# The passage between two mixtures of experts: code order, a split moved to VectorE, and drains of GpSimd

## The chip, the cores and the metric

The program runs on one core of one Trainium2 chip. The metric is the device time of one execution in microseconds (us). The kernel before took 1118.88 us in the median of three runs (1117.98 to 1119.69).

TensorE (PE in the profile, PEld for its weight loads), VectorE (DVE), ScalarE (ACT) and GpSimd (POOL) compute; SyncE (SP) issues the plain loads and stores; GpSimd issues the indirect ones, which take each row's address from a table on chip.

## The reference

Three layers follow one another. An attention with pooled keys and values makes 4608 tokens of 512 numbers. A first mixture of 8 experts sends each token to one expert by the largest of 8 logits. A second mixture does the same with its own weights and a bias per modality. An expert is two matrix products with a ReLU between them.

```python
e_idx = np.argmax(logits, axis=1)
...
for e in range(E):
    mask = e_idx == e
    h = np.maximum(x[mask] @ w1[e], 0.0)
    ye = h @ w2[e]
    out[mask] = gate_w[mask, None] * eom[mask, e, None] * ye
```

## The kernel before, in words

**Tokens and blocks.** Attention writes each token as a row into `xs1`, in the region of its expert. The first mixture (`mixture(1, ...)`) then works on blocks of 256 rows of one expert. How many blocks there are depends on the data: at least SMIN = 18, at most SMAX = 25. It scatters its results into `xs2` by the second mixture's expert, and the second mixture (`mixture(2, ...)`) works on blocks of `xs2` and scatters rows into `out`. In the profiled execution mixture 1 has 22 blocks (0 to 21) and mixture 2 has 19.

**A block** is `one(s)`. All products are made of three: weights and activations are each split into a high part (W1H, W2H, xH, HH) and a rest (W1L, W2L, xL, HL). `first_layer` makes eight groups of twelve matmuls, one per 128 columns of the hidden layer; after each two groups ScalarE writes HH[kk] (L772) and VectorE writes HL[kk] (L773). `second_layer` then runs 24 matmuls for each half of 128 tokens (L825). With its last argument true (`apart`) it runs all HH x W2H first, then HH x W2L for the first half of the hidden layer, then HL x W2H, then the rest of HH x W2L; without it, the three products of one group follow one another. A block with at most 128 tokens takes `first_layer_half` instead. ScalarE weighs the result (`weigh`, L828).

**The end of a token in mixture 1.** VectorE takes dot products with the second gate (`dots`, L853) and chooses the expert (`choose`, L868 to L881, which ends with the one-hot `oh`). `place` counts ranks with three small matmuls (L886 to L888) and works out the row (L895 to L902). `scatter` sends the rows with GpSimd's indirect DMA (L907). These steps run one block behind.

**Weights.** When the expert changes, SyncE loads raw weights into R1 and R2 ahead of time. `split1` makes W1H and W1L (ScalarE, VectorE, L192 and L193); W2H is made by ScalarE (L1062) and W2L by GpSimd (`low2`, L839, four pieces of 256 columns per tile).

**Blocks that may come.** From block 18 on, each block stands inside an `If` on a flag read from the tables, nested in the block before it (`rest`, L1092 to L1103). Its `Else` is `end(s - 1)`. So the code of all possible blocks comes first, and the eight copies of `end` stand behind them. Where both branches of an `If` advance semaphores by different amounts, the shorter one makes up for it; on GpSimd this is INC_SWDGE_SEM for indirect DMAs that were not issued.

**The passage** is `end(s)` (L1082). It splits W2 for mixture 2's first block, three tiles with ScalarE and GpSimd (`split2`, L841) and the last one in `rest` of `begin` (L974 to L976) with ScalarE and VectorE. It chooses and places the last block's tokens and runs the first layer of mixture 2's first block. `first_layer` takes a tuple `between` for this: `here` is called after group number `after` (7 of 0 to 7 in the passage), ahead of that pair's results, and `then` after the results of pair `after // 2`. `here` places and scatters the last tokens and makes counts (L222 to L228); `then` makes the block table (L160 to L189) and issues the load of block 1. The rest of block 0 of mixture 2, from its second layer on, stands in `go_on2`, behind all the copies of `end`.

The order of instructions on each engine is the order in which the program writes them. The program schedules by hand and adds semaphores where data is shared.

Of the kernel before, what the change touches and what calls it, by code (L numbers as in the profile page):

```python
# [47 lines left out]
def kernel(ctx, tc, q, k, v, wg, wo, w1, w2, mod, wg2, bias2, v1, v2, out):  # L48
# [717 lines left out]
    def first_layer(xh, xl, between=None):  # L766


        kept = []

        def results(kk, p):
            ACT.activation(HH[kk], p, AF.Relu)  # L772
            DVE.scalar_tensor_tensor(HL[kk], in0=p, scalar=0.0, in1=HH[kk].bitcast(F32), op0=ALU.max, op1=ALU.subtract)  # L773

        after, early, here, then = between or (NF, None, None, None)
        trio = [(W1H, d, xh) for d in range(ND)] + [(W1L, d, xh) for d in (0, 2, 3)] + [(W1H, d, xl) for d in range(ND)] + [(W1L, 1, xh)]
        for kk in range(NF // 2):
            p = pm.tile([P, 2 * BLK], F32, name=f"h{kk}").rearrange("p (c s) -> p c s", c=2)
            for c2 in range(2):
                f = 2 * kk + c2  # L780
                c = f * P
                for n, (W, d, x) in enumerate(trio):
                    PE.matmul(p[:, c2, :], lhsT=W[d][:, c:c + P], rhs=x[:, d, :], start=n == 0, stop=n == 3 * ND - 1)  # L783
                if f == 0 and early:
                    early()
                if f == after:
                    here()
                    for k2, p2 in kept:
                        results(k2, p2)
            if early and 2 * kk + 1 < after:  # L790
                kept.append((kk, p))
                continue
            results(kk, p)
            if kk == after // 2:
                then()

    def first_layer_half(xh, xl):
# [37 lines left out]
    def low2(part):  # L835
        for j in part:
            for c in range(2):
                for w in steps(DM):
                    GP.tensor_tensor(W2L[j][:, c, w], R2[j][:, c, w], W2H[j][:, c, w].bitcast(F32), op=ALU.subtract)  # L839

    def split2(part):  # L841
        for j in part:
            ACT.activation(W2H[j], R2[j], AF.Copy)
            low2((j,))

    bc2 = lambda t: t.unsqueeze(2).to_broadcast([P, 2, E])
    c28 = lambda t: t.unsqueeze(1).to_broadcast([P, 2, E])
# [68 lines left out]
    def mixture(m, rows, a1, a2, base, first, after):  # L916
# [44 lines left out]

            return rest

        def begin(part, early, before, of, x):

            def opening():

                before()
                counts(base, of()["eh"], ni, nf)

            def rest():
                f = of()
                if m == 2:
                    ACT.activation(W2H[3], R2[3], AF.Copy)  # L974
                    for c in range(2):
                        DVE.tensor_tensor(W2L[3][:, c], R2[3][:, c], W2H[3][:, c].bitcast(F32), op=ALU.subtract)  # L976
                else:
                    DVE.memset(xg_of(1)[:, 1, DM + 1:DM + 2], float(N))
                flag = lambda c: tc.If(reg(nf[0:1, c:c + 1], [ET.SP], 1) > 0)
                table(base, f["order"], *tabs, m)  # L980
                before = list(placed[f"xs{m}"])
                with flag(FMORE) as more:
                    apart(f"xs{m}", SP.dma_start(rows[ds(reg(nf[0:1, FEND:FEND + 1], [ET.SP], E * REG - P), P), :], dummy))
                    load_block(1, reg(f["ei"][0:1, 1:2], [ET.SP], (E - 1) * REG) + BLK, flag(FHALF2))
                placed[f"xs{m}"] = before
                with more.Else():
                    pads(rows, ni, m)
                    fetch(1)
                placed[f"xs{m}"] = before

            first_layer(*x, between=(part, early, opening, rest))

        def ahead():
            pads(rows, ni, m)
# [5 lines left out]
        def one(s):  # L1000
# [22 lines left out]
                split1()  # L1023
            if s == 0:
                p = pm.tile([P, DM], F32, name="y", bufs=2)
                second_layer(0, p)
                if m == 1:
                    turn_in(1)()
            if m == 1:
# [4 lines left out]
            if m == 1:  # L1034
# [8 lines left out]
                    DVE.tensor_tensor(w[:, 1:E], w[:, 1:E], w[:, 0:1].to_broadcast([P, E - 1, DM]), op=ALU.subtract)  # L1043
                dots(p, S, 0)
            if m == 2:
                write_out(S, 0)
            p1 = pm.tile([P, DM], F32, name="y", bufs=2)
            with half2(s, [ET.PE, ET.Activation, ET.Pool]) if s > 0 else ExitStack():  # L1048
# [11 lines left out]
            with when(s, SPLIT2, [ET.Activation, ET.Pool]):  # L1060
                for j in range(NF // 2):
                    ACT.activation(W2H[j], R2[j], AF.Copy)  # L1062
                low2(range(NF // 2))
            if m == 1 and s > 0:
                scatter()
            if m == 1 and s == SMIN - 2:
                fav["e"] = reg(fav["ei"][0:1, 0:1], [ET.SP], E - 1)
# [13 lines left out]

        def end(s):  # L1082

            split2(range(3))
            choose(RS[s % 2])

            def before():
                place(RS[s % 2], half2(s, [ET.Pool]), "t0")()

            after(NF - 1, None, before, lambda: fav, x_of(s + 1))  # L1090

        def rest(s):  # L1092
            before = {g: list(names) for g, names in placed.items()}
            with tc.If(goes_on[s] > 0) as there:
                one(s)
                if s + 1 < SMAX:
                    rest(s + 1)
                elif m == 1:
                    end(s)
            if m == 1:  # L1100
                placed.update(before)
                with there.Else():
                    end(s - 1)  # L1103

        def go_on():
            for s in range(SMIN):
# [37 lines left out]

    begin2, go_on2 = mixture(2, xs2, v1, v2, base2, lambda: M["xg20"], None)
    begin1, go_on1 = mixture(1, xs1, w1, w2, base1, lambda: xg0, begin2)
    begin1(2, last_but_one, room, lambda: dict(order=order1, ei=ei1, eh=eh1), (xH, xL))
    go_on1()
    go_on2()

# [50 lines left out]
```

## Time and profile before

| | |
|---|---|
| median of three runs | 1118.88 us |
| profiled execution, its own time | 1117.44 us |
| its span in the trace | 1115.7 us |
| TensorE busy | 1066.5 us (96%) |
| VectorE, ScalarE, GpSimd busy | 594.6, 393.8, 334.7 us |
| mean granted clock of TensorE | 0.991 |

The span runs from the first to the last instruction; the 1.7 us between it and the execution's own time lie around it. Busy time counts work on data alone: branches, register loads, semaphores, DRAIN and INC_SWDGE_SEM belong to an engine's sequencer, whose name has a q in the trace (POOLq, PEldq). The granted clock is a share of full speed. Times of instructions are us from the span's start, durations of one are in ns or us as the columns say.

### The profile page before, as it was taken

The numbers are of one execution on the slowest core, as the hardware profiler recorded it, in microseconds if no ns is written. First come the engines' busy times: TensorE is split into PE (matmuls) and PEld (weight loads), VectorE is DVE, ScalarE is ACT, GpSimd is POOL, SyncE is SP. The second block draws the span as 40 slices with busy tenths as digits, with TensorE's granted clock in tenths as the row PEclk, the third lists the DMA queues.
The fourth block names the chain that finished last, engine by engine and source line by source line (L and its number), as shares of the span: only waits on it lengthen the run. The fifth ranks groups of instructions, "written<-read, shape, count | busy, mean of one in ns | idle before, by whom it ended". The sixth has DMA issues, their size and how long they took to land. (4 is left out here: it accounts for less than half of the span.)

```text
span 1115.7 us, 21941 instructions
## 1 busy us (share of the span) xinstructions
PE 1066.5 (96%) x7058; PEld 961.6 (86%) x7058; DVE 594.6 (53%) x1839; ACT 393.8 (35%) x924; POOL 334.7 (30%) x563
## 2 busy tenths in 40 slices
PE   7998989999999999999999989999999999999993
PEld 6998888998888888888888878889998898889982
DVE  6889777768887667679866673211112222111120
ACT  6887872216354215236221151211212512111120
POOL 7566484113757215108312130011000140101000
PEclk9999999999999999999999989999999999999997
DMA  9877455613746114125511005511011211111000
GB/s 345 276 283 250 174 201 189 218 49 123 258 155 225 58 49 161 64 78 163 185 54 41 21 24 177 205 58 58 31 40 39 60 40 39 43 55 40 21 20 22
DMA packets 52096, 128.17 MB, mean 115 GB/s; under 512 B 6957, under 2 KB 10029, under 8 KB 51760
## 3 DMA queue, kind: packets, MB, share of 16 engines
q1 hardware_dynamic: 42928, 97.28, 26.7%
q0 software_dynamic: 8960, 28.47, 6.5%
q8 instruction: 88, 1.44, 0.5%
q14 instruction: 120, 0.98, 0.3%
HBM read 92.51 MB, written 34.27 MB: 114 GB/s over the span
## 5 line engine op out<-in xcount | busy, mean ns | idle before, releaser
L773 DVE SCALAR_TENSOR_TENSOR hl<-h,hh 128x512 fp32r<-128x512 f32 x140 | 95.3, 690 | 368.4 <-ACT hh L772 365.3
L825 PE MATMUL y<-W2H,hh 128*128 128x512 f32 x608 | 235.3, 398 | 2.8 <-ACT W2H L974 2.5
L825 PE MATMUL y<-W2L,hh 128*128 128x512 f32 x608 | 234.6, 395 | 0.5 <-POOL W2L L839 0.5
L825 PE MATMUL y<-W2H,hl 128*128 128x512 f32 x608 | 233.3, 395 | 0.0
L772 ACT ACTIVATE hh<-h 128x512 fp32r<-128x512 f32 x140 | 83.3, 596 | 312.4 <-PE h L783 309.2
L853 DVE CUSTOM_DVE_ANT_0 junk<-y,wg2b 128x512 f32<-128x512 f32 x273 | 169.5, 685 | 8.3 <-ACTq L1060 5.2
L828 ACT ACTIVATE y<-y,xg 128x512 f32<-128x512 f32 x76 | 52.3, 688 | 300.4 <-PE y L825 236.4
L1080 POOL DMA_INDIRECT out_dram<-y,ti x37 | 36.0, 973 | 380.1 <-ACT y L828 258.9
L825 PEld LDWEIGHTS y<-W2H,hh 128*128 128x128 f32 x608 | 114.0, 188 | 28.5 <-ACT W2H L974 2.5
L825 PEld LDWEIGHTS y<-W2H,hl 128*128 128x128 f32 x608 | 114.4, 188 | 26.8
L825 PEld LDWEIGHTS y<-W2L,hh 128*128 128x128 f32 x608 | 114.6, 188 | 26.0 <-POOL W2L L839 1.3
L839 POOL TENSOR_TENSOR W2L<-R,W2H 128x256 fp32r<-128x256 f32 x140 | 99.5, 747 | 84.5 <-ACT W2H L1062 82.2
L783 PE MATMUL h<-xH,W1L 128*128 128x256 f32 x608 | 123.7, 285 | 0.2 <-DVE W1L L193 0.2
L783 PE MATMUL h<-xH,W1H 128*128 128x256 f32 x608 | 100.4, 288 | 4.6 <-issue 3.8
L783 PE MATMUL h<-x2H,W1L 128*128 128x256 f32 x512 | 103.2, 282 | 0.1
L907 POOL DMA_INDIRECT xs<-y,qdi x39 | 39.8, 1020 | 203.3 <-DVE lg L853 190.0
L783 PE MATMUL h<-xL,W1H 128*128 128x256 f32 x608 | 98.5, 285 | 0.0
L783 PEld LDWEIGHTS h<-xH,W1L 128*128 128x128 f32 x608 | 95.8, 193 | 0.4 <-DVE W1L L193 0.4
L783 PEld LDWEIGHTS h<-xH,W1H 128*128 128x128 f32 x608 | 84.7, 194 | 5.0 <-issue 3.8
L783 PEld LDWEIGHTS h<-xL,W1H 128*128 128x128 f32 x608 | 84.6, 194 | 0.0
L783 PE MATMUL h<-x2H,W1H 128*128 128x256 f32 x512 | 83.8, 285 | 0.4 <-ACT x2H L245 0.4
L783 PE MATMUL h<-x2L,W1H 128*128 128x256 f32 x512 | 82.1, 282 | 0.0
(241 smaller groups left out, 1597.1 us busy)
## 6 DMA issues: line engine op xcount, KB each, us to landing
R<-in_w_dram SPq DMA_DIRECT2D x56, 512.0 KB, 4.7
xg<-xs SPq DMA_DIRECT2D x72, 258.0 KB, 2.7
kv<-in_v_dram SPq DMA_DIRECT2D x16, 576.0 KB, 4.5
R<-in_v_dram SPq DMA_DIRECT2D x16, 512.0 KB, 6.3
kv<-in_k_dram SPq DMA_DIRECT2D x14, 576.0 KB, 8.8
qt<-in_q_dram SPq DMA_DIRECT2D x14, 576.0 KB, 10.1
xs<-dummy SPq DMA_DIRECT2D x18, 258.0 KB, 3.5
wraw<-in_w_dram SPq DMA_DIRECT2D x8, 512.0 KB, 4.3
```

Of the source, the lines that this page charges most:

```text
L772: ACT.activation(HH[kk], p, AF.Relu)
L773: DVE.scalar_tensor_tensor(HL[kk], in0=p, scalar=0.0, in1=HH[kk].bitcast(F32), op0=ALU.max, op1=ALU.subtract)
L783: PE.matmul(p[:, c2, :], lhsT=W[d][:, c:c + P], rhs=x[:, d, :], start=n == 0, stop=n == 3 * ND - 1)
L825: PE.matmul(p, lhsT=X[f // 2][:, f % 2, hf * P:(hf + 1) * P], rhs=W[f // 2][:, f % 2, :], start=i == 0, stop=i == 3 * NF - 1)
L828: ACT.activation(S["y"][:, hf, 0:DM], p, AF.Copy, scale=S["xg"][:, hf, DM:DM + 1])
L839: GP.tensor_tensor(W2L[j][:, c, w], R2[j][:, c, w], W2H[j][:, c, w].bitcast(F32), op=ALU.subtract)
L853: DVE.tensor_tensor_reduce(out=M["junk"][:, e % 2], in0=p, in1=M["wg2b"][:, e, :], scale=1.0, scalar=0.0, op0=ALU.mult, op1=ALU.add, accum ...
L907: apart("xs2", GP.indirect_dma_start(xs2, IDX(ap=di[:, hf:hf + 1], axis=0), y[:, hf, :], None, bounds_check=E * REG - 1, oob_is_err=False))
L1080: apart("out", GP.indirect_dma_start(out, IDX(ap=S["ti"][:, hf:hf + 1], axis=0), S["y"][:, hf, 0:DM], None, bounds_check=N - 1, oob_is_err ...
```

## The change

- `rest` of mixture 1 turns its `If` round: the condition is now that there are no more blocks, `end(s - 1)` is its body, and the next block stands in the `Else`. Mixture 2's `rest` is as before.
- In `end`, ScalarE makes all four W2H tiles ahead of `choose`, and VectorE makes all of W2L, in halves of 512 columns: tiles 0 and 1 behind HL[1], tile 2 behind HL[2], tile 3 behind HL[3]. `split2` goes.
- `here` of the passage runs after group 5 instead of 7; `then` runs after pair 3, as before, which is now an argument of its own. For mixture 1's own first block nothing moves.
- The second layer of mixture 2's block 0 runs with the parts apart for its first half of tokens.
- GpSimd gets a `drain` in each block: in mixture 1 from block 1 on ahead of the scatter, in mixture 2 ahead of the first write-out.

```diff
-        after, early, here, then = between or (NF, None, None, None)
+        after, early, here, then_at, then, each = between or (NF, None, None, None, None, None)
...
             results(kk, p)
-            if kk == after // 2:
+            if each:
+                each(kk)
+            if kk == then_at:
                 then()
...
                 f = of()
-                if m == 2:
-                    ACT.activation(W2H[3], R2[3], AF.Copy)
-                    for c in range(2):
-                        DVE.tensor_tensor(W2L[3][:, c], R2[3][:, c], W2H[3][:, c].bitcast(F32), op=ALU.subtract)
-                else:
+                if m == 1:
                     DVE.memset(xg_of(1)[:, 1, DM + 1:DM + 2], float(N))
...
-                second_layer(0, p)
+                second_layer(0, p, m == 2)
...
             if m == 2:
+                GP.drain()
                 write_out(S, 0)
...
             if m == 1 and s > 0:
+                GP.drain()
                 scatter()
...
         def end(s):
 
-            split2(range(3))
+            for j in range(NF // 2):
+                ACT.activation(W2H[j], R2[j], AF.Copy)
             choose(RS[s % 2])
+
+            def each(kk):
+                for j in {1: (0, 1), 2: (2,), 3: (3,)}.get(kk, ()):
+                    for c in range(2):
+                        DVE.tensor_tensor(W2L[j][:, c], R2[j][:, c], W2H[j][:, c].bitcast(F32), op=ALU.subtract)
...
-            after(NF - 1, None, before, lambda: fav, x_of(s + 1))
+            after(5, None, before, lambda: fav, x_of(s + 1), 3, each)
 
         def rest(s):
-            before = {g: list(names) for g, names in placed.items()}
-            with tc.If(goes_on[s] > 0) as there:
+            if m == 2:
+                with tc.If(goes_on[s] > 0):
+                    one(s)
+                    if s + 1 < SMAX:
+                        rest(s + 1)
+                return
+
+            names = lambda: {g: list(n) for g, n in placed.items()}
+            before = names()
+            with tc.If(goes_on[s] < 1) as stop:
+                end(s - 1)
+            ended = names()
+            placed.update(before)
+            with stop.Else():
                 one(s)
                 if s + 1 < SMAX:
                     rest(s + 1)
-                elif m == 1:
+                else:
                     end(s)
-            if m == 1:
-                placed.update(before)
-                with there.Else():
-                    end(s - 1)
+            placed.update(ended)
```

## Rows read from the trace of the kernel before

**Rows 1.** The page, busy time of each engine.
```profile
PE 1066.5 (96%) x7058; PEld 961.6 (86%) x7058; DVE 594.6 (53%) x1839; ACT 393.8 (35%) x924; POOL 334.7 (30%) x563
```
**Rows 2.** What TensorE waited for: us in total, times, longest us.
```profile
PE h L783 <- issue: 3.8, 1, 3.8
PE y L825 <- ACT W2H L974: 2.5, 1, 2.5
```
**Rows 3.** By stretch: us; PE, PEld, DVE, ACT, POOL busy (x); PEclk; DMA; GB/s.
```profile
649.70:653.40 3.70, 0.00 (x0) 0.01 (x1) 3.67 (x11) 0.73 (x2) 0.00 (x0) 0.84 0.02 7
653.40:667.70 14.30, 14.28 (x99) 14.17 (x99) 11.04 (x31) 4.87 (x8) 10.47 (x14) 0.80 0.12 43
667.70:670.20 2.50, 0.04 (x2) 0.04 (x1) 2.43 (x20) 1.51 (x2) 0.99 (x1) 1.00 0.01 3
670.20:681.40 11.20, 11.20 (x48) 9.07 (x49) 4.99 (x37) 0.69 (x1) 0.98 (x1) 1.00 0.36 120
```
**Rows 4.** TensorE in order of time, mixture 2's block 1: start us, us.
```profile
682.89 0.99 PE L783 MATMUL h<-x2H,W1H 128*128 128x256 f32 x4 [0.44 <-ACT x2H L245]
...
694.75 0.40 PE L825 MATMUL y<-W2H,hh 128*128 128x512 f32 x1
```
**Rows 5.** TensorE's branches, lines 1094 (640 to 680) and 1011: ns min/median/max, first, last start.
```profile
L1094 PEldq COMPARE_BRANCH  x2: 3394/3616/3838, 649.9 to 666.3; - x2
...
L1011 PEldq COMPARE_BRANCH  x72: 65/169/437, 191.4 to 1087.9; - x72
```
**Rows 6.** The program's closing line 1196, from 1099 on.
```profile
L1196 SPq EVENT_SEMAPHORE  x14: 17/28/28, 1105.5 to 1115.7; - x14
...
L1196 POOLq DRAIN  x3: 46/107/9223, 1105.7 to 1115.5; - x3
L1196 SPq DRAIN  x3: 7/7/13, 1106.2 to 1115.2; - x3
```
**Rows 7.** Line 1094 from 1100 on.
```profile
L1094 POOLq INC_SWDGE_SEM  x1: 2408/2408/2408, 1103.1 to 1103.1; - x1
```
**Rows 8.** The program's opening line 1187.
```profile
L1187 POOLq DRAIN  x1: 169/169/169, 0.4 to 0.4; - x1
```
**Rows 9.** GpSimd: line 906; line 907 up to 307.5; its indirect DMAs with idle time.
```profile
L906 POOLq INC_SWDGE_SEM  x5: 1074/1295/1660, 307.5 to 668.9; - x5
...
L907 POOL DMA_INDIRECT xs<-y,qdi x8: 967/1021/1066, 216.3 to 300.2; - x8
...
L907 POOL DMA_INDIRECT xs<-y,qdi x39 | 39.8, 1020 | 203.3 <-DVE lg L853 190.0 <-issue 5.4 <-DVE ft L138 2.5
L497 POOL DMA_INDIRECT xs<-x,rdi x36 | 36.2, 1005 | 48.5 <-DVE nm L385 22.1 <-DVE lgs L438 12.2 <-issue 6.2
L1080 POOL DMA_INDIRECT out_dram<-y,ti x37 | 36.0, 973 | 380.1 <-ACT y L828 258.9 <-ACTq L1060 76.2 <-DVE ti L1032 45.0
```
**Rows 10.** GpSimd in order of time: second split of a pair, idle before it.
```profile
522.22 11.26 POOL L839 TENSOR_TENSOR W2L<-R,W2H 128x256 fp32r<-128x256 f32 x16 [0.97 <-SPq L1073]
```
**Rows 11.** VectorE in order of time, the end of block 21 and the passage.
```profile
645.35 0.36 DVE L874 SCALAR_TENSOR_TENSOR qlg<-lg,y,bs 128x8 f32<-128x8 f32 x2
...
646.78 0.17 DVE L881 TENSOR_TENSOR oh<-qa,va 128x16 bf16<-128x16 f32 x1
...
657.99 0.08 DVE L853 DVE_READ_ACCUMULATOR2_ANT lg<- 128x1 f32 x1
...
667.78 0.16 DVE L895 TENSOR_TENSOR qdd<-t,base 128x16 f32<-128x16 f32 x1
...
669.34 0.68 DVE L773 SCALAR_TENSOR_TENSOR hl<-h,hh 128x512 fp32r<-128x512 f32 x1
669.94 1.28 DVE L976 TENSOR_TENSOR W2L<-R,W2H 128x512 fp32r<-128x512 f32 x2
```
**Rows 12.** SyncE's load of block 1, second half; the page, loads to landing (us).
```profile
675.54 0.33 SPq L935 DMA_DIRECT2D xg<-xs  x1
...
xg<-xs SPq DMA_DIRECT2D x72, 258.0 KB, 2.7
```

More of the change, by code (lines that the diff above doesn't have):

```diff
@@ L839, in low2 @@
                     GP.tensor_tensor(W2L[j][:, c, w], R2[j][:, c, w], W2H[j][:, c, w].bitcast(F32), op=ALU.subtract)
[L841 to L844, printed above, removed]
     bc2 = lambda t: t.unsqueeze(2).to_broadcast([P, 2, E])
@@ L962, in turn_in, with begin @@
             return rest
-        def begin(part, early, before, of, x):
+        def begin(part, early, before, of, x, then_at, each=None):
             def opening():
@@ L989, in rest @@
                 placed[f"xs{m}"] = before
-            first_layer(*x, between=(part, early, opening, rest))
+            first_layer(*x, between=(part, early, opening, then_at, rest, each))
         def ahead():
@@ L1146 @@
     begin1, go_on1 = mixture(1, xs1, w1, w2, base1, lambda: xg0, begin2)
-    begin1(2, last_but_one, room, lambda: dict(order=order1, ei=ei1, eh=eh1), (xH, xL))
+    begin1(2, last_but_one, room, lambda: dict(order=order1, ei=ei1, eh=eh1), (xH, xL), 1)
     go_on1()
```

## The prediction, made before the changed kernel ran

> **What bounds the kernel now.** I began with the page's busy times. TensorE is busy for 96% of the span [rows 1], so outside the two ends of the program only its idle stretches are worth anything. The list of what TensorE waited for shows which of them lie where the diff works [rows 2]: one of 3.75 us put down to issue, ahead of the first layer (L783), and one of 2.46 us ahead of the second layer (L825), put down to a ScalarE copy of W2H[3]. Both stand in the passage from mixture 1 to mixture 2.
>
> The table by stretch [rows 3] gives the passage its shape. From 649.7 to 653.4 TensorE does nothing. Then mixture 2's first layer takes 14.3 us with a granted clock of 0.80, against 11.86 us for the same 96 matmuls one block later, at full clock [rows 4]. Then come 2.5 us of nothing at clock 1.00.
>
> The branch records say what the idle stretches are [rows 5]. TensorE's two branches at L1094 took 3394 and 3838 ns: the first is the jump from the end of block 21 to the far copy of `end`, the second the jump from there to the code of mixture 2. A jump over one half of a block's code (L1011) takes 65 to 437 ns. So I don't believe the releaser W2H L974: the matmul started at 670.16, just when the jump that began at 666.3 was over (666.3 + 3.84). The sequencer stood 1.4 us ahead of the array there, since the last matmul ended at 667.7; that is why 3.84 us show as 2.46.
>
> Last the tail. GpSimd's final DRAIN lasts 9223 ns and starts at 1105.7, so it ends at 1114.9; the span ends 0.8 us later. SyncE had finished its own waits, 0.8 us of them, by 1106.3, and they began at 1105.5 [rows 6], just as GpSimd's INC_SWDGE_SEM of 2408 ns, started at 1103.1, ended [rows 7].
>
> **The drains.** Each adds one instruction on GpSimd per block: 21 before a scatter of mixture 1, 19 before the first write-out of mixture 2. Do they shorten the last one? A DRAIN at the start, with no indirect DMA before it, took 169 ns [rows 8]. INC_SWDGE_SEM took 1074 ns at 307.5, behind 36 + 8 indirect DMAs, and 2408 ns at the end, behind 36 + 39 + 37 = 112 [rows 9]: 1334 ns over 68 of them, 19.6 ns each, on a floor of 211 ns. At 668.9, behind 74, that line gives 1661 ns, and the longest of that row's five, the one there, is 1660. Something piles up with each indirect DMA. After the 9223 ns DRAIN the next two took at most 107 ns, so a DRAIN clears what it works on. I take it as clearing that pile: (9223 - 169) / 112 = 81 ns for each.
>
> With a drain per block, two indirect DMAs are left at the end. INC_SWDGE_SEM then takes 211 + 2 x 20 = 250 ns, and SyncE is released at 1103.35 and done at 1104.2. The last DRAIN takes 169 + 2 x 81 = 330 ns from 1103.55. The later is SyncE: 1104.2 + 0.8 = 1105.0 against 1115.7, a gain of **10.7 us**. The bounds: nothing, if the last drain stays; 8.6 us, if the drain shrinks but INC_SWDGE_SEM does not, since SyncE then still ends at 1106.3. I take the upper value because the two durations grow with the same count.
>
> What do the 40 drains themselves cost? About 0.33 us each, and 169 + 36 x 81 ns = 3.1 us the first time. Behind the drain waits the scatter, which GpSimd reaches early anyway: its scatters sat idle for 190.0 us on VectorE's dots and its write-outs for 258.9 us on ScalarE's y [rows 9]. The narrow place is a block in which W2 is split while the next split follows at once: there GpSimd had 0.97 us to spare [rows 10]. 0.33 us fits. Cost: nothing while a drain stays below about 1 us.
>
> **The passage.** `end` now follows the branch directly, so the first far jump becomes a fall-through. That removes 3.75 us of idle and the lower clock behind it, 14.3 - 11.86 = 2.4 us. It also takes twelve splits of W2L off GpSimd; VectorE gets eight halves of W2L at 0.64 us each [rows 11] instead of two.
>
> I run the new order forward. TensorE starts the first layer at 649.9 and needs 11.86 / 8 = 1.48 us per group of 128 columns, so six groups end at 658.8. The placing matmuls now stand there, and they need `oh`. VectorE ends its dots at 658.07, and `choose` takes 1.6 us where GpSimd splits nothing beside it [rows 11], so `oh` is there at 659.9: a new wait of 1.2 us. Two more groups end at 663.0. The far jump to mixture 2's code stays: 3.84 us less the 1.4 us of lead leaves 2.4, and the second layer starts at 665.5 instead of 670.2.
>
> Is VectorE in time? After 659.9: two HL (0.68 each), four halves of W2L to 663.8, placing and counts (1.56) to 665.4, HL[2], W2L[2], HL[3], W2L[3] to 669.3. The second layer's matmuls take 0.23 us (48 in 11.2 us [rows 3]). The order with parts apart wants HL[3] after eighteen of them, at 669.6, and W2L[3] after 22, at 670.6. Ready at 668.0 and 669.3, both are in time, by over 1 us. So the gain is **4.7 us**. What is late next is mixture 2's block 1: its second load was issued at 675.54 and lands 2.7 us after issue [rows 12]. It waits for the last scatter, which moves forward with the placing by about 4 us, so it lands near 674.3, ahead of its transposes at 676.7.
>
> Bounds of the jump's exposed part: 0 us from below (then W2L[3] limits, and 0.9 us more is gained) and all 3.84 us, plus a lower clock, from above. Idle of 3.75 us was followed by the lower level (1.2 GHz), idle of 2.46 us was not [rows 3]; mine is 2.4 us with 1.2 us shortly before, so I take no drop. The drop's price: 3.7 x 0.16 / 0.5 + 14.3 x 0.20 / 0.5 = 6.9 us at that level, which costs up to 3.4 us if TensorE has work throughout.
>
> Blocks 18 to 21 now jump over `end` once each. That is about the size of a half of a block's code, so 65 to 437 ns [rows 5], inside the sequencer's lead of 1.4 us: nothing. If the lead were gone, 1.7 us for the four.
>
> **Sum.** 10.7 + 4.7 = 15.4 us off the profiled execution's 1117.44 us, 1102.0. The median of the runs shown is 1118.88, 1.44 above it, so I expect **1103.5 us**.
>
> **Rivals.** First, the jump's stall brings the lower clock in the second layer: 1103.5 + 3.4 = 1106.9. For it speaks that 2.4 us is near the idle that did it; against it, that 2.46 us did not. Second, INC_SWDGE_SEM counts something a drain leaves alone: 1105.6. Third, the drains do not do that: the last DRAIN keeps its length and only the passage gains, 1118.88 - 4.7 = 1114.2. Against this stands the growth with the count. This is the place of a rule in the Trainium skill, VectorE: DVE Perf Modes, section The DRAIN you can't avoid: the DRAINs that the runtime adds take about 12 ns, constant, on all five engines. SyncE's agree (7 to 13 ns), GpSimd's 9223 ns does not; by that rule there would be nothing to shorten. Fourth, the passage gains nothing because the jump loses its lead and the clock falls: 1108.2.
>
> On the other side: a drain behind an indirect DMA has a fixed price of 9.2 us. In the pairs of blocks that both split W2 [rows 10], the second split would start 9.2 - 0.97 = 8.2 us late and TensorE would wait for W2L. Two such pairs give 16.4 us; 1118.88 - 4.7 + 16.4 = 1130.6, slower. It decides from about 1 us per drain. Against it: the two short drains at the end.
>
> **Chances.** Forecast 0.47, lower clock 0.22, INC unchanged 0.14, passage nothing 0.05, tail unchanged 0.06, fixed price 0.03; 0.03 for what I don't see. The range 1101.5 to 1109.5 holds the first four; its low end is the forecast less 0.9 us for a hidden jump and the 0.9 us by which the lowest run lies under the median, rounded down. A measurement can tell about 0.2% from no change, 2.2 us: all cases but the fixed price lie beyond that on the fast side, so faster 0.95, same 0.02, slower 0.03.
>
> **What would show it.** Right: the last GpSimd DRAIN under 0.5 us and INC_SWDGE_SEM near 250 ns everywhere; only one branch over 3 us on TensorE near 650 to 670; no idle ahead of the first layer, and clock 1.00 there; a new wait of about 1.2 us of the placing matmul for `oh`. Wrong: a last DRAIN of several us, per-block drains of several us, `W2L` or `hl` as what ends a wait of the second layer, or a clock below 1 behind the jump.

## The result, and the profile after

The changed kernel takes **1104.36 us** in the median of four runs (1103.42 to 1104.71); the kernel before took 1119.29 beside it (1117.98 to 1121.37, four runs). The ratio is **0.9861 [0.9841, 0.9881]**: faster, 14.9 us off by the medians. The profiled execution took 1104.66 us, its span is 1103.0 us against 1115.7.

The spans differ by 12.7 us and the medians by 14.9. The profiled execution of before, 1117.44 us, lay 1.85 us under the median of before, that of after 0.3 us above its own. What follows accounts for the 12.7.

**The tail.** First the closing line 1206 of the changed kernel and the last instructions of line 1095 (columns: engine and operation, count, ns min/median/max, first and last start); they answer to [rows 6, 7].

```profile
L1095 POOLq COMPARE_BRANCH  x3: 38/40/45, 1073.5 to 1100.4; - x3
...
L1095 POOLq INC_SWDGE_SEM  x1: 215/215/215, 1100.1 to 1100.1; - x1
...
L1206 SPq DRAIN  x3: 7/7/13, 1101.1 to 1102.4; - x3
L1206 POOLq DRAIN  x3: 46/111/301, 1101.8 to 1102.7; - x3
```

The last DRAIN takes 301 ns instead of 9223, INC_SWDGE_SEM 215 instead of 2408. SyncE is through with its waits at 1101.1. GpSimd's DRAIN starts at 1101.8, though its branch was taken at 1100.4: with these 1.4 us GpSimd, and not SyncE, is now the last to arrive. GpSimd in order of time, its last write-out in both kernels, before first:

```profile
1098.59 0.97 POOL L1080 DMA_INDIRECT out_dram<-y,ti  x1 [4.60 <-ACTq L1060]
```
```profile
1096.42 0.97 POOL L1075 DMA_INDIRECT out_dram<-y,ti  x1 [4.60 <-ACTq L1054]
```

From there to the end of the span it was 17.1 us and is 6.6 us: 10.5 us.

**The passage.** The changed kernel by stretch, columns as in [rows 3]:

```profile
651.84:652.27 0.43, 0.00 (x1) 0.03 (x1) 0.43 (x2) 0.43 (x1) 0.00 (x0) 1.00 0.00 0
652.27:661.14 8.87, 8.87 (x72) 8.76 (x73) 8.47 (x30) 5.31 (x8) 2.03 (x2) 1.00 0.16 62
661.14:662.22 1.08, 0.00 (x1) 0.00 (x0) 0.95 (x7) 0.70 (x2) 0.00 (x0) 1.00 0.00 0
662.22:665.40 3.18, 3.18 (x27) 2.97 (x26) 3.18 (x6) 0.00 (x0) 0.00 (x0) 1.00 0.02 5
665.40:666.87 1.47, 0.00 (x2) 0.01 (x1) 1.44 (x15) 0.60 (x1) 0.00 (x0) 1.00 0.02 6
666.87:678.16 11.29, 11.29 (x48) 9.07 (x49) 7.82 (x46) 0.69 (x1) 0.97 (x1) 1.00 0.30 97
```

The 3.7 us ahead of the first layer are 0.43 us, the clock is 1.00 throughout, six groups run through, then comes the new wait of 1.08 us (for `oh`) and the remaining jump with 1.47 us. TensorE's branches at line 1103 between 640 and 690 (for [rows 5]):

```profile
L1103 PEldq COMPARE_BRANCH  x2: 73/1810/3547, 652.0 to 663.3; - x2
```

One jump of 3547 ns is left. It starts at 663.3, 2.1 us before the array runs out of work at 665.40; 3.55 - 2.1 is the 1.47 that shows.

To size the passage I take TensorE from the last placing of block 21 to the second layer of mixture 2's block 1. TensorE in order of time, before, then after:

```profile
280.85 0.18 PE L886 MATMUL h<-oh,tri_b 128*128 128x16 bf16 x1 [0.91 <-DVE oh L881]
...
649.44 0.18 PE L886 MATMUL h<-oh,tri_b 128*128 128x16 bf16 x1
...
681.41 1.03 PE L241 MATMUL t<-ident,xg 128*128 128x128 f32 x8
```
```profile
280.46 0.18 PE L883 MATMUL h<-oh,tri_b 128*128 128x16 bf16 x1 [0.91 <-DVE oh L878]
...
651.61 0.18 PE L883 MATMUL h<-oh,tri_b 128*128 128x16 bf16 x1
...
678.16 1.03 PE L241 MATMUL t<-ident,xg 128*128 128x128 f32 x8
...
681.44 1.10 PE L783 MATMUL h<-x2L,W1H 128*128 128x256 f32 x4 [0.23 <-DVE x2L L252]
...
692.59 0.39 PE L827 MATMUL y<-W2H,hh 128*128 128x512 f32 x1
```

To block 1's transposes the passage is 26.55 us instead of 31.97, 5.4 us less. Of these, 1.1 are given back within block 1: its second layer starts 40.98 us after the placing, against 694.75 [rows 4] - 649.44 = 45.31. Net **4.3 us**. The wait for `x2L` in it comes from VectorE, which is itself late in mixture 2's code (VectorE in order of time, after):

```profile
680.63 0.17 DVE L1025 CAST ti<-xg 128x2 int32<-128x2 f32 x1 [5.73 <-DVEq L1015]
```

The 5.73 us lie behind two branches: 2.8 us from the far one (L1103, 674.89) to VectorE's next record, and 2.4 us behind a near one (L1015, 678.10). In the kernel before, the same two places took 3.4 and 0.2 us. Why the near branch is slow here stays open.

**A loss ahead of it.** TensorE reaches block 21's placing at 651.61 instead of 649.44, 2.2 us late. Sum: -10.5 - 4.3 + 2.2 = -12.6 of the 12.7 us. The drains' own row (line 1059, mixture 1) shows where to look, with GpSimd in order of time under it, all after:

```profile
L1059 POOLq DRAIN  x21: 121/223/8469, 191.4 to 640.8; - x21
```
```profile
280.17 1.06 POOL L904 DMA_INDIRECT xs<-y,qdi  x1 [1.16 <-DVE qkm L876]
```

Of the 21 drains, 13 take 0.1 to 0.2 us. The first takes 3.0 us, behind the 36 indirect DMAs of attention, as forecast (3.1). The seven that stand behind splits of W2 take 8.4 to 8.5 us, since they wait for GpSimd's own work; there the scatter starts 1.16 us after the last piece of W2L. Besides, the clock fell twice to its lower level of 1.2 GHz (by stretch, after; the granted clock is the third number from the right):

```profile
282.00:285.40 3.40, 3.40 (x19) 3.40 (x18) 3.40 (x7) 0.15 (x1) 3.11 (x6) 0.51 0.92 307
517.60:521.00 3.40, 3.40 (x19) 3.40 (x18) 3.40 (x7) 0.00 (x0) 3.06 (x7) 0.50 0.96 284
```

The drains of mixture 2 (line 1039, after) are long too:

```profile
L1039 POOLq DRAIN  x19: 305/2230/7851, 675.5 to 1074.5; - x19
```

There a drain follows closely on the write-out of the block ahead, and it ends 0.1 us after that write-out has landed (688.64 behind 688.52, 732.47 behind 732.35, 1051.98 behind 1051.87); the longest, 7.9 us, stands behind splits of W2. They cost nothing that shows: GpSimd's next write-out starts 4 to 15 us after the drain's end, and from block 1's second layer to the last write-out the two kernels take the same 403.8 us.

### The profile page after: what moved, and what is told of

It reads as the page before. It is cut to its first block, busy times and chain, and to the rows that moved or that the text cites. A ratio compares the mean times of both kernels' runs of the same rounds, so it can differ in the third digit from the quotient of the medians.

```text
span 1103.0 us, 21979 instructions
## 1 busy us (share of the span) xinstructions
PE 1066.7 (97%) x7058; PEld 962.2 (87%) x7058; DVE 594.2 (54%) x1845; ACT 393.4 (36%) x924; POOL 324.9 (29%) x551
## 5 line engine op out<-in xcount | busy, mean ns | idle before, releaser
L841 POOL TENSOR_TENSOR W2L<-R,W2H 128x256 fp32r<-128x256 f32 x128 | 91.8, 753 | 78.7 <-ACT W2H L1056 76.9
L904 POOL DMA_INDIRECT xs<-y,qdi x39 | 39.8, 1021 | 218.5 <-DVE lg L850 160.6
```

What stands on the lines that cost most here:

```text
L904: apart("xs2", GP.indirect_dma_start(xs2, IDX(ap=di[:, hf:hf + 1], axis=0), y[:, hf, :], None, bounds_check=E * REG - 1, oob_is_err=False))
```

## Experiments

There are three groups, each on another chip and beside the kernel before, which took 1118.40 us there (e1 to e4), 1119.41 (e5 to e8) and 1118.21 (c1, c2, e9, e10). Across groups the ratios are to be compared rather than the medians.

| run | edit | median | ratio to before |
|---|---|---|---|
| e1_drains_alone | before + drains | 1107.54 | 0.9905 [0.9890, 0.9921] |
| e2_passage_alone | changed - drains | 1112.55 | 0.9945 [0.9932, 0.9959] |
| e3_drains_in_2 | changed - drains of mixture 1 | 1103.04 | 0.9863 [0.9848, 0.9878] |
| e4_far_end | changed, old code order | 1109.43 | 0.9913 [0.9896, 0.9929] |
| e5_one_drain | one drain in all | 1105.84 | 0.9880 [0.9863, 0.9896] |
| e6_w2l_gpsimd | W2L on GpSimd again | 1107.49 | 0.9894 [0.9878, 0.9911] |
| e7_place_later | e3, placing after group 7 | 1105.24 | 0.9872 [0.9856, 0.9889] |
| e8_second_layer_ahead | e3, half a second layer ahead of the jump | 1105.32 | 0.9874 [0.9857, 0.9890] |
| c1_changed_again | changed | 1104.30 | 0.9875 [0.9855, 0.9895] |
| c2_drains_in_2_again | as e3 | 1103.18 | 0.9863 [0.9844, 0.9882] |
| e9_order_alone | drains and code order alone | 1106.94 | 0.9901 [0.9881, 0.9922] |
| e10_drain_ahead | mixture 1's drain ahead of the splits | 1103.29 | 0.9861 [0.9841, 0.9880] |

### The two halves of the change, each alone

```diff
 # e1: the kernel before
             if m == 1 and s > 0:
+                GP.drain()
                 scatter()
...
             if m == 2:
+                GP.drain()
                 write_out(S, 0)
 # e2: the changed kernel, the same two lines taken out
```

> The kernel before with nothing but the two drains (one ahead of each scatter of mixture 1, one ahead of each first write-out of mixture 2). Theory: a drain clears what each indirect DMA leaves behind, so the last DRAIN falls from 9.22 to about 0.3 us and the last INC_SWDGE_SEM from 2.41 to about 0.22 us, and the tail from the last write-out to the end of the span falls from 17.1 to 6.6 us: 1119.3 - 10.5 = 1108.8 us. Rival: in the blocks that split W2 the drain takes 8.4 us because it waits for GpSimd's own splits, and this holds something up; then part of the 2.2 us by which TensorE reaches the end of block 21 later in the changed kernel belongs to the drains and the time is 1110 to 1111. Second rival: that loss is the clock falling to the lower level for 3.4 us at two places by chance, which a new profile need not show at the same places.

> The changed kernel without the drains. Theory: the tail of 17.1 us is back (last DRAIN 9.2 us, INC_SWDGE_SEM 2.4 us), the passage is as in the changed kernel: 1104.4 + 10.5 = 1114.9 us, that is 4 to 5 us below the kernel before. TensorE reaches the second layer of mixture 2's first block as early after block 21 as with the drains. Rival: the drains cost 1 to 2 us in mixture 1's blocks, then this gives 1113 to 1114. Second rival: the passage's gain needs the drains (the scatters come sooner): 1119.

Measured 10.9 us below before for the drains and 5.9 for the passage. The closing line's DRAIN of e1, then of e2, and e2's last INC_SWDGE_SEM:

```profile
L1198 POOLq DRAIN  x3: 46/107/208, 1104.3 to 1105.4; - x3
```
```profile
L1093 POOLq INC_SWDGE_SEM  x1: 2418/2418/2418, 1100.7 to 1100.7; - x1
...
L1204 POOLq DRAIN  x3: 46/107/9223, 1103.3 to 1113.1; - x3
```

The drains alone make the tail short, and without them it is back to the nanosecond (9223). The two halves don't need each other. 10.9 + 5.9 is 1.9 us more than the 14.9 of both, and e2 lay 2.4 us under its expectation; the changed kernel's own ratio was 0.9861 beside one group and 0.9875 in another, 1.6 us, so what hangs on 1 or 2 us is read from the traces. In e2 the passage, measured as above, takes 40.65 us (691.92 - 651.27), 4.7 less than before.

### How a drain's price grows

```diff
 # e5: the changed kernel, no drain in mixture 1
             if m == 2:
-                GP.drain()
+                if s == 2:
+                    GP.drain()
                 write_out(S, 0)
```

> One drain in the whole kernel, in mixture 2's third block, ahead of its first write-out; the passage as changed. Theory: a DRAIN takes about 0.1 us and 81 ns for each indirect DMA since the last one, INC_SWDGE_SEM about 0.2 us and 19.6 ns for each. With 75 + 4 indirect DMAs ahead of it the one drain takes 6.5 us, hidden; 37 - 4 = 33 are left for the end, so the last DRAIN takes 2.8 us and the last INC_SWDGE_SEM 0.85 us, in all 3.1 us more at the end than with a drain per block: 1103.0 (the run with drains in mixture 2 alone) + 3.1 = 1106.1 us. Rival: what a drain clears does not grow one by one with the indirect DMAs but is a table that is filled to a bound; then the last DRAIN is either 0.3 or 9.2 us, and the time 1103 or 1113.

Measured 1105.84 us, 2.8 above e3 by the medians and 1.8 when each is set against the kernel before of its group; in the traces the end behind the last write-out is 3.2 us longer than in e3 (9.4 against 6.2). Its one drain, its last INC_SWDGE_SEM and its closing DRAIN:

```profile
L1040 POOLq DRAIN  x1: 6528/6528/6528, 705.7 to 705.7; - x1
...
L1095 POOLq INC_SWDGE_SEM  x1: 838/838/838, 1099.9 to 1099.9; - x1
...
L1206 POOLq DRAIN  x3: 52/107/2754, 1100.9 to 1104.2; - x3
```

6.53, 0.84 and 2.75 us against 6.5, 0.85 and 2.8 expected: both prices grow with each indirect DMA, and a drain anywhere earlier clears both. The last write-out of e5 had landed at 1098.3, 2.6 us before its closing DRAIN began, so those 2.75 us are no wait for a transfer. The table with a bound falls. The first drain of mixture 2 in e3, behind 75 indirect DMAs, fits too: 6202 ns, or (6202 - 169) / 75 = 80 ns each. Row of e3, 673 to 700:

```profile
L1039 POOLq DRAIN  x2: 4056/5129/6202, 674.5 to 683.6; - x2
```

### What the passage's gain is made of

```diff
 # e4: rest() of mixture 1 as before; everything else as changed
-            with tc.If(goes_on[s] < 1) as stop:
-                end(s - 1)
+            with tc.If(goes_on[s] > 0) as there:
+                one(s)
...
+                with there.Else():
+                    end(s - 1)
 # e6: W2L on GpSimd; each() goes
             for j in range(NF // 2):
                 ACT.activation(W2H[j], R2[j], AF.Copy)
+            low2(range(NF // 2))
             choose(RS[s % 2])
 # e9: as e6, and the placing behind the whole first layer
-            after(5, None, before, lambda: fav, x_of(s + 1), 3)
+            after(NF - 1, None, before, lambda: fav, x_of(s + 1), 3)
```

> The changed kernel with the code order of before (the blocks that may come directly behind the branch, the end far away), all else as changed: VectorE's splits and the early placing stay. Theory: the code order is what the passage gains: the jump to the far end again leaves TensorE idle for some 3.3 us ahead of the first layer, the granted clock falls behind it (2.4 us more), and the new wait for oh (1.08 us) goes: 1104.4 + 3.3 + 2.4 - 1.1 = 1109.0 us. Rival: the gain is VectorE's splitting in GpSimd's place and the earlier placing, and the order of the code alone moves nothing: 1104.4 to 1105.4.

> The changed kernel with W2L of mixture 2's first block split by GpSimd, as before, and not by VectorE; code order, placing and drains as changed. Theory: VectorE's part is no gain by itself, it only makes room: GpSimd is free from 659 and its 16 quarters of 0.70 us would be done at 670.4, ahead of the need (671.5); choose gets slower beside it, so the wait for oh grows from 1.1 to some 1.8 us: 1104.4 + 0.7 = 1105.1 us. Rival: the scatter of the last block queues behind the splits, the load of mixture 2's second block lands 3 us later and TensorE waits for its transposes: 1106 to 1108. Other rival: VectorE with 5 us less to do is early everywhere and the kernel is faster, 1103.5.

> The drains and the new code order alone: W2L by GpSimd and the placing behind the whole first layer, as before. Theory: GpSimd's splits beside VectorE make oh ready only 13.2 us after the first layer starts (as in the run with GpSimd's splits), so TensorE waits 1.4 us behind the 11.9 us of the first layer; the jump to mixture 2's code starts only then and shows in full, 3.4 us: the second layer starts 16.9 us after the first, against 14.6 us as changed: 1104.4 + 2.3 = 1106.7 us. Rival: order is all that counts, and VectorE's splits and the early placing only keep the balance: 1104.4. Other rival: as slow as GpSimd's splits with the early placing, 18.2 us: 1108.

e4 came out at 1109.43 us (1109.0 expected): without the new code order the passage gains nothing. From block 21's placing to block 1's second layer e4 takes 44.67 us (697.32 - 652.65), and so does e1 (695.95 - 651.28), which has the drains alone. TensorE in order of time, then by stretch, in e4:

```profile
656.69 1.20 PE L783 MATMUL h<-xH,W1H 128*128 128x256 f32 x4 [3.81 <-issue]
```
```profile
656.00:663.00 7.00, 6.31 (x30) 6.34 (x31) 5.25 (x23) 4.50 (x5) 2.04 (x2) 0.51 0.22 81
```

The far jump is back with 3.81 us, and the clock at 0.51 for 7 us behind it.

e6 missed by 2.4 us, on the slow side of all its cases. TensorE's waits in e6 from 655 to 675, and VectorE in order of time:

```profile
PE t L883 <- DVE oh L878: 4.4, 1, 4.4
```
```profile
663.98 1.50 DVE L871 SCALAR_TENSOR_TENSOR qlg<-lg,y,bs 128x8 f32<-128x8 f32 x2 [0.33 <-DVEq L1052]
665.51 0.17 DVE L872 TENSOR_REDUCE qm<-qlg 128x2 f32<-128x16 f32 x1
...
668.24 0.65 DVE L878 TENSOR_TENSOR oh<-qa,va 128x16 bf16<-128x16 f32 x1
```
```profile
662.57 11.09 POOL L841 TENSOR_TENSOR W2L<-R,W2H 128x256 fp32r<-128x256 f32 x16
```

`choose` takes 4.9 us (663.98 to 668.89) beside GpSimd's splits, against 1.6 without them (660.57 to 662.17 in the changed kernel). Its steps with two tiles as inputs grow, such as L878 from 0.17 to 0.65 us; its reductions stay at 0.17. The Trainium skill, SBUF — State Buffer, section SBUF: two separate sides, has that as a lock on a shared port pair, which a VectorE instruction with two SBUF inputs and a GpSimd instruction that reads SBUF take in turn; the trace agrees, with the 0.17 us reductions as the control. So the move to VectorE is worth 3 us here, and not for VectorE's speed: it keeps GpSimd's splits out of the time in which `oh` is made. Right behind the 4.4 us the granted clock stood at 0.54 for 3.5 us, which costs little, since the slower matmuls cover the jump behind them (0.32 us of it show).

e9 came out as expected (1106.94 against 1106.7): 1.62 us for `oh`, and then the whole jump of 3427 ns, since nothing is queued behind the placing. TensorE in e9, in order of time and by stretch:

```profile
664.40 0.17 PE L883 MATMUL t<-oh,tri_b 128*128 128x16 bf16 x1 [1.62 <-DVE oh L878]
...
668.04 3.78 PE L827 MATMUL y<-W2H,hh 128*128 128x512 f32 x8 [3.42 <-issue]
```
```profile
668.04:672.00 3.96, 3.96 (x9) 3.13 (x10) 3.82 (x22) 0.00 (x0) 2.02 (x3) 0.50 0.17 57
```

The two groups behind the placing in the changed kernel are what gives TensorE's sequencer its lead at the jump. By the measure above, beside drains throughout, the code order alone (e9, 44.24 us) is worth 0.4 us, the order with the early placing (e6, 43.51) 1.2, the early placing and VectorE's split without the order (e4) nothing, and all three together (40.98) 3.7.

### What the drains of mixture 1 cost

```diff
 # e3, c2: the changed kernel
             if m == 1 and s > 0:
-                GP.drain()
                 scatter()
 # e10: the changed kernel
+            if m == 1 and s > 0:
+                GP.drain()
             with when(s, SPLIT2, [ET.Activation, ET.Pool]):
...
             if m == 1 and s > 0:
-                GP.drain()
                 scatter()
```

> The changed kernel without the 21 drains of mixture 1; the first drain of mixture 2 then clears some 74 indirect DMAs at once. Theory: that drain takes 169 + 74 x 81 ns = 6.2 us, hidden behind the wait for the first y of mixture 2 or showing up to 1 us, everything after it is as in the changed kernel, INC_SWDGE_SEM in mixture 1 is long again (1 to 1.7 us, off the path): 1104.4 us, within 1 us. Rival: the 8.4 us drains in the seven blocks that split W2 hold work up, then this is 1 to 2 us faster: 1102.4 to 1103.4. Other rival: the 6.2 us drain delays the first write-out so that a y buffer is not free: 1 to 3 us slower.

> The changed kernel as it is, on the same chip as the next three. Theory on where 2.2 us went ahead of the passage: in mixture 1 each pair of blocks that both split W2 loses 0.8 to 1.4 us at TensorE. Either the drain behind GpSimd's own splits holds GpSimd for about 1 us, the next split and with it oh come later and TensorE waits for oh once more (0.3 to 0.7 us); or the clock falls for 3.4 us at the first block of the pair (1.0 to 1.2 us), and then the wait for oh is gone because TensorE is late itself. So TensorE reaches the end of block 21 again 1.5 to 2.8 us late against the first block, whether or not the clock falls. Rival: it was the clock alone, by chance; without a fall of the clock near 282 and 517 nothing is lost. Time: within 1.5 us of 1104.4.

> Again the kernel with drains in mixture 2 alone. Theory: without drains in mixture 1 the two pairs lose only what a fall of the clock costs, so this is 1 to 2 us faster than the changed kernel on the same chip if no clock falls there, and level with it if it falls at both. Rival: no difference in the medians (under 0.5 us), as the first comparison had it.

> The changed kernel with mixture 1's drain ahead of the splits of W2 in its block and not behind them. Theory: what a drain costs in mixture 1 is the restart of GpSimd behind its own splits (1.16 us of idle ahead of the scatter against 0.15 without a drain). Ahead of the splits it takes 0.2 us in a time in which GpSimd waits for ScalarE's W2H, so no DRAIN of 8.4 us is left, the scatter follows the last split by 0.2 us, the additional wait for oh in each pair is gone and the time is that of drains in mixture 2 alone. Rival: the drain there waits for the scatter's and the biases' work of the block ahead and holds the split up by as much: no gain over the changed kernel.

c1 shows no fall of the clock near 282 or 517, and yet the loss. TensorE in c1, in order of time:

```profile
280.93 0.18 PE L883 MATMUL h<-oh,tri_b 128*128 128x16 bf16 x1 [0.91 <-DVE oh L878]
...
536.99 0.18 PE L883 MATMUL h<-oh,tri_b 128*128 128x16 bf16 x1 [0.67 <-DVE oh L878]
...
651.46 0.18 PE L883 MATMUL h<-oh,tri_b 128*128 128x16 bf16 x1
```

The same in c2, and GpSimd in c2 ahead of the scatter:

```profile
281.99 0.18 PE L883 MATMUL h<-oh,tri_b 128*128 128x16 bf16 x1 [0.91 <-DVE oh L878]
...
650.43 0.18 PE L883 MATMUL h<-oh,tri_b 128*128 128x16 bf16 x1
```
```profile
299.89 1.07 POOL L904 DMA_INDIRECT xs<-y,qdi  x1 [0.17 <-issue]
```

From the first of these placings to that of block 21: 368.59 us in the kernel before (649.44 - 280.85), 370.53 in c1, 368.44 in c2. So the drains of mixture 1 cost 2 us here. The other kept traces say how firm that is. Without these drains, and with no fall of the clock near 282 or 517, the stretch takes 368.6 (before), 368.4 (c2) and 368.6 us (e3). With the drains behind the splits and no fall there it takes 369.6 (e1), 370.3 (e9), 370.5 (c1), 370.8 (e6) and 371.3 us (e4): a cost of 1.0 to 2.7 us. A fall there without such drains (e2, e5, e7) gives 369.5 to 369.6, so the changed kernel's first profile, 371.15 us, holds both. e8 has neither and takes 369.5; 0.6 us of it lie between 558 and 583, from a cause that was not looked for.

The loss lies in the pairs of blocks that both split W2. While a DRAIN waits for the splits, GpSimd's sequencer can't run ahead: the register moves of the scatter (L904), which start at 272.3 and 273.0 in c2, during the splits, start at 279.7 and 280.5 in c1, behind them, and the scatter 1.17 us after the last piece instead of 0.15. Then the next block's splits are late as well. In the second pair the first placing is at the same time (516.25 in c1, 516.27 in c2); the next splits on GpSimd and the start of `choose` on VectorE, c1 first, then c2:

```profile
524.27 11.26 POOL L841 TENSOR_TENSOR W2L<-R,W2H 128x256 fp32r<-128x256 f32 x16 [1.33 <-ACT W2H L1056]
531.66 4.03 DVE L871 SCALAR_TENSOR_TENSOR qlg<-lg,y,bs 128x8 f32<-128x8 f32 x2
```
```profile
523.15 11.30 POOL L841 TENSOR_TENSOR W2L<-R,W2H 128x256 fp32r<-128x256 f32 x16 [0.83 <-SPq L1067]
531.67 2.94 DVE L871 SCALAR_TENSOR_TENSOR qlg<-lg,y,bs 128x8 f32<-128x8 f32 x2
```

`choose` starts at the same time in both, but its first step ends only 0.16 us after GpSimd's last piece (535.69 behind 535.53, 534.61 behind 534.45). It is held up as in e6, so a split that ends 1.1 us later makes `oh` 1.1 us later, and TensorE waits 0.67 us for it.

Ahead of the splits the drain costs little: e10 takes 368.9 us over the same stretch. The drains of e10:

```profile
L1055 POOLq DRAIN  x21: 120/205/3022, 194.7 to 642.6; - x21
```

None of 8.4 us is left. e10's median is 1103.29 us and c2's 1103.18, beside c1's 1104.30: in the order that was expected, by 1.0 to 1.1 us, but the intervals of the ratios overlap, so that the medians alone would not show it. With the traces, drains in mixture 2 alone, or ahead of the splits, are the better version of the change. In e10 one additional wait for `oh` of 0.34 us stayed, at 539.2.

### Two tries for more

```diff
 # e7: e3 with
-            after(5, None, before, lambda: fav, x_of(s + 1), 3, each)
+            after(6, None, before, lambda: fav, x_of(s + 1), 3, each)
 # e8: e3 with, behind that call,
+            p = pm.tile([P, 2 * BLK], F32, name="t1")
+            second_layer(0, p, True)
+            weigh(p, 0, dict(RS[0], xg=M["xg20"]))
```

> The kernel with drains in mixture 2 alone, with the placing matmuls behind the seventh group of the first layer and not the sixth. Theory: the 1.08 us wait for oh goes, since the seventh group takes 1.48 us, and VectorE, still at W2L by then, is not held up: 1103.0 - 1.1 = 1101.9 us. Rival: the second layer, 1.1 us earlier, then waits for hl[3] or W2L[3], or the jump to mixture 2's code shows by 1.1 us more: 1103.0.

> The kernel with drains in mixture 2 alone, with the second layer of mixture 2's first block (first half) and the weighing of its rows moved ahead of the jump to mixture 2's code. Theory: the 1.3 to 1.5 us that TensorE idles ahead of the second layer are the part of the 3.4 us jump that its sequencer's lead does not cover; behind matmuls of 512 columns (0.23 us each, against 0.12 us for 256) the same number of instructions of lead is about 4 us, so the jump is hidden: 1103.0 - 1.4 = 1101.6 us. Rival: VectorE's hl[3] and W2L[3] are just in time now, and take the place of the idle: 1102.5 to 1103.0. Other rival: ScalarE's own jump, now behind the weighing, delays x2H of the second block: 1103 to 1106.

Neither gained: their ratios, 0.9872 and 0.9874, lie above the 0.9863 of e3. TensorE in order of time, in e7 (its weight loads, PEld, and line 903 between 660 and 675 under it) and then in e8:

```profile
669.00 2.07 PE L827 MATMUL y<-W2L,hh 128*128 128x512 f32 x4 [3.05 <-DVE W2L L1085]
```
```profile
669.00 0.50 PEld L827 LDWEIGHTS y<-W2L,hh 128*128 128x128 f32 x2 [3.48 <-POOLq L1102]
```
```profile
L903 POOLq INC_SWDGE_SEM  x1: 1657/1657/1657, 667.2 to 667.2; - x1
```
```profile
672.41 0.79 PE L827 MATMUL y<-W2H,hh 128*128 128x512 f32 x1 [3.21 <-issue]
```

In e7 the 1.1 us for `oh` went, and 3.05 us ahead of the first matmul on W2L came, longer than the rival had it. The first two rows name two releasers. VectorE's piece is one by chance: the pieces of the tile that this matmul reads were done by 662.61. The weight load waits on a semaphore of GpSimd as well, which GpSimd advances at L1102, where it makes up for the branch not taken, at 668.96. That stands behind the scatter of the placing and its INC_SWDGE_SEM, 1657 ns here, since e7 has no drains in mixture 1, and 222 in the changed kernel. e3 shows the same in small: its weight load waits 0.78 us for L1102, the changed kernel's doesn't wait. So e7 doesn't say what the later placing is worth with drains in mixture 1; by the two durations some 1.4 us of the wait would be gone and the rest would stay, an estimate that was not run. In e8 the jump of 3497 ns began at 668.9, only 0.3 us before the array ran out of work (672.41 - 3.21 = 669.2): behind a wait of 0.19 us for `hl` at 667.5 TensorE's sequencer was not ahead of the array. The lead of 4 us that I worked out from a count of instructions was wrong. VectorE is busy for 14.5 of the 15.0 us between block 21 and the second layer in the changed kernel (the first five stretches above). So little more can be had there unless VectorE has less to do; that is a conclusion from the busy time and was not tried.

## Why the prediction was right, point by point

1103.5 us was predicted, 1104.36 measured. Two terms held; a cost of 1 to 3 us was put at nothing; and that the total came out so close is luck, since the base of the sum erred the other way.

- **The tail, 10.7 us predicted, 10.5 by the trace.** The last DRAIN was put at 330 ns and took 301, INC_SWDGE_SEM at 250 and took 215; e1, e2 and e5 show the cause. Not in the sum: GpSimd's 1.4 us between its last branch and the closing line, which makes GpSimd and not SyncE the later one. The rivals "INC unchanged" and "the drains do not do that" fall. With the latter goes the rule of the Trainium skill (VectorE: DVE Perf Modes, The DRAIN you can't avoid) for GpSimd's first closing DRAIN: 301 ns in the changed kernel and 9223 in the one before, no constant.
- **The passage, 4.7 us predicted, 4.3 by the trace.** The order (e4), the placing and VectorE's splits (e6, e9) worked as described, but only together. The wait for `oh` was put at 1.2 us and took 1.08. The jump's exposed part was put at 2.4 and was 1.47, because the lead was 2.1 us and not 1.4, and the jump 3.55 and not 3.84: the step "3.84 us less the 1.4 us of lead" was mis-sized by 0.9. Against it stand 1.1 us in block 1. There the step that failed was "what is late next": I named the load of block 1, and it was VectorE's own 5.73 us of idle behind its branches, which I had costed only on TensorE.
- **The clock** stayed at 1.00 behind the jump's 1.47 us, and fell in e4, e6, e7, e8 and e9 behind 3.81, 4.39, 3.05, 3.21 and 3.42 us: the first rival's mechanism is real, and the 1.47 us here did not bring it about.
- **"Blocks 18 to 21 now jump over `end`: nothing"** held: the four jumps take TensorE 328 to 343 ns, and c2, in which they stand, needs 368.4 us up to block 21's placing, the kernel before 368.6. Another branch of TensorE in block 21 grew with the new order (L1004, 1352 ns at 636.5, against 341 before), and the lead hides it too.
- **"0.33 us fits. Cost: nothing"** failed. It counted a drain's own time, and what a drain takes behind queued splits is the sequencer's lead: GpSimd starts again only 1.16 us after its last piece. The slack of 0.97 us [rows 10] does not absorb that (GpSimd's idle there is 1.33 us in c1), the next splits come 1.1 us later, and so does `oh`. c1 against c2 shows 2.1 us lost, all profiles together 1.0 to 2.7. In mixture 2 the drains took 2.2 us in the median and not 0.33, for nothing, since GpSimd waits there anyway: the sign "per-block drains of several us" came, and the mechanism held all the same. The rival on the slow side had the place right (pairs that split twice) and the point from which it decides ("about 1 us"); its price of 9.2 us was wrong, since of the 8.4 us that show most is GpSimd's own work.
- **The base.** On the profiled executions I said 1102.0 and it was 1104.66, 2.7 us more: 2.2 from what was lost ahead of block 21's placing (the drains, and the two falls of the clock in that profile), 0.4 from the passage, the rest from the tail. Adding 1.44 us for the median hid that, by luck: the profiled execution before lay below its median, and the one after did not.
- **Two of its sums don't come out.** 658.07 + 1.6 is 659.7 and not 659.9 (the trace after has 0.33 us between dots and `choose`, which the sum lacks), and by its own times a hidden jump would give 670.6 - 669.3 = 1.3 us before W2L[3] limits, not 0.9. Neither moves the forecast or the range by more than 0.4 us.

## What to carry to other kernels

Where GpSimd issues many indirect DMAs, look at the DRAIN and INC_SWDGE_SEM in which the program ends: a drain in a place where GpSimd waits anyway moves that cost off the end (the later it stands, the less is left), and it belongs ahead of GpSimd's work in a block, not behind it. Put the code that is taken at a hand-over directly behind its branch, keep matmuls without waits between the last semaphore and a far jump, and cost that jump on every engine that makes it. Before moving work between VectorE and GpSimd, look at what short VectorE instructions run beside it.

## What the runs showed of the hardware

- GpSimd's DRAIN costs some 80 ns and INC_SWDGE_SEM some 20 ns for each indirect DMA since the last drain (DRAIN: 2.75 us for 33, 3.02 for 36, 6.20 for 75, 6.53 for 79, 9.22 for 112). Close behind an indirect DMA a DRAIN lasts until 0.1 us after that DMA has landed.
- Where GpSimd's scatter had nothing else to wait for, it started 0.88 to 0.93 us after the DRAIN's end, behind short drains (0.2 us) as behind long ones (8.4 us): the sequencer's steps ahead of it come after the DRAIN and not during GpSimd's work.
- A VectorE step with two tiles as inputs (L871) ended 0.16 us after GpSimd's last split in c1 and in c2, whether it had started 2.9 or 4.0 us earlier.
- The granted clock fell for 3.4 us behind some 1.9 us of idle in short pieces (0.24, 0.91 and 0.70 us, near 280) in the changed kernel's first profile, and did not in its second, with the same pieces (0.25, 0.91, 0.70). Near 282 or 517 it fell in e2, e5 and e7 as well, which have no drains there, and in no other profile. In this kernel such a fall is no property of the code, and 1 us of a comparison of two profiles can be that.
